# One projection slot fewer is shared: the left stage, the gates and the left rows move into other buffers

## The chip, the core and the metric

The kernel runs on one core of one Trainium2 chip. Its engines work side by side: PE (TensorE: matmuls, with PEld for its weight loads), DVE (VectorE), ACT (ScalarE), POOL (GpSimd) and SP (SyncE, which here only issues DMAs). SBUF is the large on-chip memory, PSUM the matmuls' own with 8 banks of 512 fp32 columns on 128 partitions. The metric is the device time of one execution in microseconds (us), the median of several runs; lower is better.

## The reference, cut to what matters

`x` has 2048 rows of 640, cut into 64 segments of 32 rows. A memory of 8 rows is handed from segment to segment:

```python
for s in range(64):
    h = concatenate([mem, x[32 * s:32 * s + 32]])      # 40 rows
    q, k, v = h @ Wq, h @ Wk, h @ Wv                   # 32 heads of 192
    p = softmax(where(mask, q @ k.T * 192 ** -0.5, -1e9))
    o = (p @ v) @ Wo
    mem, out_s = o[:8], o[8:]
a = concatenate(out)                                   # 2048 x 640
b = (gelu(x @ w_gate) * (x @ w_up)) @ w_down           # a feed-forward of its own
g = sigmoid((x * gate_w).sum(-1))
result = g * a + (1 - g) * b
```

Segment s + 1 can't begin its projections before segment s has produced `mem`. Wq, Wk, Wv are 640 x 6144, Wo is 6144 x 640, all in bf16.

## The kernel before, in words

**Stages.** The first 177 us compute the feed-forward `b` (kept in a scratch tensor in DRAM), the gates `g`, and load the attention's weights. Then come the 64 segments, one after the other, some 25 us each.

**Weights.** The weights are cut into pieces: Wq, Wk and Wv into 5 row blocks (k0 to k4) times 4 octets of heads, 384 KB each; Wo into 16 of 480 KB. Not all fit into SBUF. So 14 projection slots (`NSQ = 14`: Q's k1 to k4, K's and V's k0 to k4) and 3 Wo slots are shared by two pieces: that of octet 0 and that of octet 3. A segment with even s takes the octets in the order 0, 1, 2, 3, one with odd s in the order 3, 2, 1, 0. So what a segment uses last, the next one uses first; in between the first octet's pieces are replaced by the last octet's (`swap_loads`, L597 issues them on SP as soon as PE has read the old piece). "Octet i" below means the i-th that a segment takes. 17 such swaps run per segment, all on SP's queue in the order of the program.

**Left rows.** A segment's input on PE has 32 columns, but mem and rows are 40. The first 24 rows and the 8 memory rows are projected in the segment. The last 8 rows ("left" rows) of four segments, a group, are projected together as 32 rows, one group ahead: in segments with s % 4 = 0, 1, 2 stand "left units", each the Q and K projection of one octet (`lf`: matmuls, L882 for Q and L226 for K; `le`: evacuation, `left_rows`: ACT L887 copies the rows from PSUM to a buffer, DVE L889 transposes them, once for Q and once for K; `left_store`, L893, stores them to a DRAM scratch). Types 0 and 2 have one unit, type 1 has two. The segment of s % 4 = 3 projects left rows of V for the next group (`vb`). I call s % 4 the **type** of a segment. Groups run out at the end: segments 60 to 63 have no left units.

**One segment.** The order is written out by hand in a list, `PROG`: projections `g` (Q, K, V of octet i; L1039, and L226 where the weights already in PE serve again), row evacuations on ACT (L1059) and transposes on DVE (`tq`, `tk`, L1073), scores (`sc`: mask L1080, L1088, L1093), softmax (DVE L1107, L1109, ACT L1119, DVE L1121 to L1126), the transposes of p (`pt`, L1139 and L1144), P times V (`pv`, L1172 and L1174; evacuated by ACT L1183 into one of two head-output buffers `uT`), and the output projection `wo` (L1201; for the last octet L1224). ACT L1207 and DVE L1210 sum the halves of the first three octets' output. DVE L1340 adds the last octet's, and L1344 transposes the new memory rows into the next segment's input; PE's first L1039 of the next segment waits for it. POOL copies left rows of Q and K into the score operands before each octet (`left_fill`, L936 and L938) from the stage `stg`, which one DMA per segment fills (`stg_load`, L932, 192 KB, issued after the scores of octet 3). `mix` (POOL L963, L968, DVE L970) blends with `b` by the gates, held in SBUF (`gall`, `gallL`); `mix_left` (POOL L963, L976, DVE L978) does so for left rows, once per group, in the next type 0 segment.

**What orders the work.** Each operation declares the regions it reads and writes; a recording layer (`_Sched`) turns overlaps into semaphore waits. Every engine's stream, SP's too, runs in program order. For a region in PSUM (a whole bank) a read also waits for earlier reads by other engines.

## Time and profile before

| | |
|---|---|
| runs | 1800.49 us median of 3 (1795.53 to 1804.5) |
| profiled execution: span, first to last instruction | 1783.4 us |
| granted TensorE clock | 0.998 |
| segment 0 starts | 176.9 us |
| mean length of a segment of type 0, 1, 2, 3 (segments 4 to 62) | 25.07, 25.56, 23.90, 25.35 us |
| DMA bytes moved | 524.33 MB, 294 GB/s |

The page tells no other time of the profiled execution than its span. Lengths of segments are read off the timeline, from the first projection matmul (L1039) of one segment to that of the next. In the views of waits each line names the engine and line that stood idle, what ended the wait, the us in total, how often, and the longest. A line of the timeline gives start and duration in us, engine, line, what is written and read, how many instructions are merged, and in brackets the idle time before and what ended it.

### The profile page before, as it was taken

What the parts mean: (1) busy time and instruction counts of PE and PEld (TensorE: products, weight loads), DVE (VectorE), ACT (ScalarE), POOL (GpSimd) and SP (SyncE); (2) the same over time, 40 slices, a digit from 0 to 9 for tenths busy, and PEclk for the clock granted to TensorE, in tenths of its full rate; (3) what the DMA queues carried; (4) which work ended last, traced back from release to release, by engine and by line L of the source; (5) the groups of instructions that cost most, each with busy time, mean ns of one, the idle gap of its engine ahead of it and who ended that gap; (6) DMA issues with size and microseconds to landing.
All of it is one profiled execution on the core that took longest, in us unless ns stands there. A gap on an engine that the chain in (4) does not pass through costs nothing.

```text
span 1783.4 us, 80070 instructions
## 1 busy us (share of the span) xinstructions
PE 1629.5 (91%) x39162; PEld 817.9 (46%) x31501; DVE 957.7 (54%) x2932; ACT 793.8 (45%) x1835; POOL 319.8 (18%) x1099
## 2 busy tenths in 40 slices
PE   9999989899998999899899999899999989899987
PEld 4554444454444444454444444454444444454443
DVE  2223555555555655555565655555555655555554
ACT  3222444444444444444444444444444544444443
POOL 1100111111211111111111111111211111111211
PEclk9999999999999999999999999999999999999999
DMA  9815887888788887888788887888888887888786
GB/s 332 297 45 177 329 318 266 324 322 316 289 295 298 318 311 261 318 318 315 287 299 299 311 319 263 322 310 319 298 299 300 317 290 269 321 313 321 289 303 260
DMA packets 263390, 524.33 MB, mean 294 GB/s; under 512 B 97384, under 2 KB 116224, under 8 KB 263040
## 3 DMA queue, kind: packets, MB, share of 16 engines
q1 hardware_dynamic: 259912, 516.11, 79.5%
q8 instruction: 276, 4.52, 1.0%
q10 hardware_dynamic: 3128, 3.09, 0.5%
q14 instruction: 74, 0.61, 0.1%
HBM read 498.00 MB, written 21.11 MB: 291 GB/s over the span
## 4 chain that ended last, share of the span: by engine, by line
PE 69%; DMA 13%; DVE 8%; ACT 6%; issue 4%; SPq 0%; DVEq 0%; ACTq 0%
PE ps L1039 20%; PE ps L226 15%; PE ps L1201 8%; DMA arena<-in_A_Wv_dram 7%; PE ps L1172 3%; DMA left_qk_scratch<-arena 3%; PE ps L802 3%; PE ps L799 3%; PE ps L882 3%; DVE arena L889 3%; PE ps L1093 2%; PE ps L817 2%; ACT arena L887 2%; PE ps L1080 2%; PE ps L1088 2%
## 5 line engine op out<-in xcount | busy, mean ns | idle before, releaser
L1039 PE MATMUL ps<-arena 128*32 128x384 bf16 x9940 | 734.8, 328 | 58.5 <-DVE arena L1344 40.4
L226 PE MATMUL ps<-arena 128*32 128x384 bf16 x7680 | 584.4, 326 | 10.8 <-ACT arena L887 6.1
L1039 PEld LDWEIGHTS ps<-arena 128*32 128x32 bf16 x9940 | 254.0, 96 | 420.1 <-issue 244.4
L1073 DVE STREAM_TRANSPOSE arena<-arena 128x384 bf16<-128x384 bf16 x512 | 279.0, 564 | 227.0 <-ACT arena L1059 226.6
L1059 ACT ACTIVATE arena<-ps 128x384 bf16<-128x384 f32 x512 | 236.2, 489 | 176.3 <-PE ps L1039 164.4
L1201 PE MATMUL ps<-arena 128*32 128x320 bf16 x6144 | 297.0, 300 | 16.1 <-issue 15.5
L1201 PEld LDWEIGHTS ps<-arena 128*32 128x32 bf16 x6144 | 163.6, 97 | 75.7 <-issue 26.5
L1119 ACT ACTIVATE ps<-ps 104x160 f32<-104x160 f32 x256 | 74.3, 290 | 236.4 <-DVE ps L1109 236.4
L1107 DVE TENSOR_REDUCE arena<-ps 104x4 f32<-104x160 f32 x256 | 83.1, 325 | 176.0 <-PE ps L1093 175.7
L1157 ACT ACTIVATE arena<-ps 128x448 bf16<-128x448 f32 x192 | 104.8, 546 | 143.3 <-PE ps L1144 143.3
L1191 POOL COPY arena<-arena 128x96 bf16<-128x96 bf16 x256 | 68.4, 267 | 522.6 <-ACT arena L1183 419.3
L936 POOL COPY arena<-arena 128x96 bf16<-128x96 bf16 x256 | 70.0, 274 | 498.7 <-PE ps L1093 436.3
L1183 ACT ACTIVATE arena<-ps 128x480 bf16<-128x480 f32 (+1 forms) x256 | 138.1, 540 | 34.0 <-PE ps L1174 29.0
L1062 ACT ACTIVATE arena<-ps 128x384 bf16<-128x384 f32 x256 | 124.8, 488 | 52.7 <-PE ps L1039 52.4
L1172 PE MATMUL ps<-arena 128*64 128x160 bf16 x1536 | 122.1, 243 | 10.4 <-issue 3.4
L1172 PEld LDWEIGHTS ps<-arena 128*64 128x64 bf16 x1536 | 80.6, 109 | 97.9 <-ACT arena L1157 46.6
L882 PE MATMUL ps<-arena 128*32 128x384 bf16 x1280 | 111.1, 330 | 1.2 <-issue 1.2
L1174 PE MATMUL ps<-arena 128*64 128x64 bf16 x1536 | 105.1, 194 | 5.8 <-issue 5.8
L1121 DVE TENSOR_REDUCE arena<-ps 104x4 f32<-104x160 f32 x256 | 81.8, 320 | 51.6 <-ACT ps L1119 43.9
L889 DVE STREAM_TRANSPOSE arena<-arena 128x384 bf16<-128x384 bf16 x128 | 73.8, 577 | 57.4 <-ACT arena L887 52.6
L1224 PE MATMUL ps<-arena 128*32 128x160 bf16 x3072 | 77.1, 234 | 22.2 <-DMA arena<-in_A_Wo_dram 12.6
L887 ACT ACTIVATE arena<-ps 128x384 bf16<-128x384 f32 x128 | 62.4, 490 | 67.6 <-DVE arena L889 38.5
(84 smaller groups left out, 1816.7 us busy)
## 6 DMA issues: line engine op xcount, KB each, us to landing
arena<-in_A_Wk_dram SPq DMA_DIRECT2D x335, 384.0 KB, 7.7
arena<-in_A_Wv_dram SPq DMA_DIRECT2D x335, 384.0 KB, 9.4
arena<-in_A_Wq_dram SPq DMA_DIRECT2D x272, 384.0 KB, 5.6
arena<-in_A_Wo_dram SPq DMA_DIRECT2D x205, 480.0 KB, 7.4
left_qk_scratch<-arena SPq DMA_DIRECT2D x64, 192.0 KB, 2.6
arena<-left_qk_scratch SPq DMA_DIRECT2D x63, 192.0 KB, 7.8
ffn_b_scratch<-arena ACTq DMA_DIRECT2D x16, 160.0 KB, 3.7
arena<-ffn_b_scratch SPq DMA_DIRECT2D x64, 40.0 KB
```

The costliest lines, as they stand in the source:

```text
L226: return e.add_instruction(mybir.InstMatmult(name=nm, start_tensor_calc=like["start"], stop_tensor_calc=stop, tile_size=(128, 32), tile_po ...
L882: fns.append(lambda e, outp=outp, rhs=rhs, j=j: e.matmul(outp, lhs, rhs, start=(k == 0), stop=(k == KT - 1), tile_position=(0, 32 * j)))
L889: S_.add("dve", lambda e: e.transpose(out=dst[:, :, m].rearrange("p q c i -> p c q i"), in_=rowl.rearrange("p (c r) -> p c r", r=L)), read ...
L1039: fns.append(lambda e, outp=outp, rhs=rhs, j=j: e.matmul(outp, lhs, rhs, start=(k == 0), stop=(k == KT - 1), tile_position=(0, 32 * j)))
L1059: S_.add("act", lambda e, m=m, bk=bk: e.activation(out=rows_sb[m], in_=ps[:, bk, 0:384], func=ACTF.Copy), reads=[r_ps[bk]], writes=[r_rows ...
L1062: S_.add("act", lambda e, i=i, bk=bk: e.activation(out=v_sb[i % NVB].rearrange("p (c n) -> p c n", c=3), in_=ps[:, bk, 0:384].rearrange("p ...
L1073: S_.add("dve", lambda e: e.transpose(out=dst[:, :, 0:L], in_=rows_sb[m].rearrange("p (c r) -> p c r", r=L)), reads=[r_rows[m]], writes=[r ...
L1157: S_.add("act", lambda e: e.activation(out=PT, in_=ps[:, bank, 0:PTW + 128], func=ACTF.Copy), reads=[r_ps[bank]], writes=[r_PT], name="pT ...
L1172: return [lambda e: e.matmul(full, v[:, e0:e0 + 64], PTm[:, i], start=True, stop=False, tile_position=(0, 64 * i), skip_group_check=True), ...
L1174: lambda e: e.matmul(part, vl[:, e0:e0 + 64], PTl[:, i], start=False, stop=True, tile_position=(0, 64 * i), skip_group_check=True)]
L1183: S_.add("act", lambda e: e.activation(out=apx(u[:, 0, 0, :], [[R, na], [3 * R, 4], [1, R]]), in_=ps[:, A, 0:na * W].rearrange("p (c t r) ...
L1201: fns.append(lambda e, i=i, t=t, j=j, gv=gv: e.matmul(ps[32 * j:32 * j + 32, bank, 0:2 * DJ].rearrange("p (h n) -> p h n", h=2), lhs2[i], ...
```

## The change

- `NSQ` goes from 14 to 13: both pieces of Q's k1 are resident, and 13 projection pieces instead of 14 are swapped per segment. The room comes from the buffers below.
- The stage `stg` is gone. Its 192 KB are loaded in two halves of 96 KB into the two `uT` buffers: half 0 after the Wo matmuls of octet 2 (`("wo", 2, 1)`), half 1 at the very end of the segment, after the left store of type 0. The fills of octets 0 and 1 read half 0, those of 2 and 3 half 1.
- The gates `gall`, `gallL` lie in columns 384 to 479 of PSUM bank 7 instead of SBUF. `gate_cols` writes them with 3 transposes and 12 copies on DVE (before: 2 and 6). A new ACT copy per segment, `gate_now`, fetches the segment's column (in type 2 also the left group's) into SBUF; it stands after the evacuation of `pv` 3.
- The left rows' buffer `rowl` is gone. The rows pass through buffers that are idle just then (`spare_buf`); with the orders used, the second V buffer, and K's buffer for the K rows of type 0.
- The left inputs: one buffer `XL` for the Q and K units instead of two, and one, `XLx`, for V's left rows inside the last left-V buffer, so that each group's left x is loaded twice.
- `mix_left` is cut in two: POOL's part (`scale_left`) runs late in type 3, DVE's stays.
- `PROG` becomes four lists, one per type, which hold what the one list gave each type, in the same order.

The core of the diff:

```diff
-    NSQ = 14
+    NSQ = 13
...
+    def half_at(s_, h):
+        return wsB_off["uT"] + h * UB
+
+    def stage(s_, i):
+        o_ = i if s_ % 2 == 0 else NOCT - 1 - i
+        at = half_at(s_, i // 2) + 4 * LW * (o_ % 2)
+        return bview(at, 4 * LW).rearrange("p (m c i) -> p m c i", m=2, i=M), r_uT[i // 2]
...
-        for ga, ra, gi, ri in ((gall, r_gall, gin, r_gin), (gallL, r_gallL, ginL, r_ginL)):
-            S_.add("dve", lambda e, ga=ga, gi=gi: e.transpose(out=ga[0:32], in_=gi[0:32]), reads=[ri[0]], writes=[ra], name="gate T")
-            for j in range(1, 4):
-                S_.add("dve", lambda e, ga=ga, j=j: e.tensor_copy(out=ga[32 * j:32 * j + 32], in_=ga[0:32]), reads=[ra], writes=[ra],
+        for n, (gi, ri) in enumerate(((gin[:, 0:32], r_gin), (gin[:, 32:64], r_gin), (ginL, r_ginL))):
+            S_.add("dve", lambda e, gi=gi: e.transpose(out=gtmp[0:32], in_=gi[0:32]), reads=[ri[0]], writes=[r_gtmp], name="gate T")
+            for j in range(4):
+                S_.add("dve", lambda e, n=n, j=j: e.tensor_copy(out=ps[32 * j:32 * j + 32, GB, GC + 32 * n:GC + 32 * n + 32], in_=gtmp[0:32]),
+                       reads=[r_gtmp], writes=[r_ps[GB]], name="gate copy")
...
-    def stg_load(s):
-        S_.add(AUXQ, lambda e: e.dma_start(stg_flat, qkl[s]), reads=[Rg("qk", NSEG * i + s, NSEG * i + s + 1) for i in range(NOCT)],
-               writes=r_stg, dma_sem="stg", name="stg s%d" % s)
+    def stg_load(s, h):
+        o0 = 2 * ((h + s) % 2)
+        at = half_at(s, h)
+        S_.add(AUXQ, lambda e: e.dma_start(bview(at, 8 * LW), qkl[s][:, 2 * LW * o0:2 * LW * (o0 + 2)]),
+               reads=[Rg("qk", NSEG * i + s, NSEG * i + s + 1) for i in (o0, o0 + 1)],
+               writes=[r_uT[h]], dma_sem="stg%d" % h, name="stg s%d" % s)
...
+    def gate_now(s):
+        two = s % 4 == 2
+        col = ps[:, GB, GC + s:GC + s + 1]
+        at = bass.AP(col.tensor, col.offset, [list(col.ap[0]), [NSEG + s // 4 - s, 2]]) if two else col
+        S_.add("act", lambda e: e.activation(out=gcur[:, 0:1 + two], in_=at, func=ACTF.Copy), reads=[r_ps[GB]],
+               writes=r_gcur[0:1 + two], name="gate s%d" % s)
...
+    gate_at = [max(("pv", NOCT - 1), ("wo", 2, 1), key=prog.index) for prog in PROGS]
...
+    def spare_buf(x):
+        at = (wsB_off["uT"] + UB, wsB_off["v"] + 768, wsB_off["K"], wsB_off["uT"])[x]
+        return bview(at, 768), sreg(at, 768)
...
-        elif s + 1 < NSEG:
-            stg_load(s + 1)
...
+            if item == gate_at[q]:
+                gate_now(s)
             swap_loads(s, item)
+            if item == ("wo", 2, 1) and s + 1 < NSEG:
+                stg_load(s + 1, 0)
...
+            if n == nqkv and q == 3:
+                scale_left(g)
...
             wo_left(s, held)
             if s + 1 == NSEG:
                 left_sums(g)
+        if s + 1 < NSEG:
+            stg_load(s + 1, 1)
```

## The prediction, on record before the changed kernel ran

> **What bounds the kernel now.** I read the page first (which engine is full), then TensorE's own waits, then the timeline around one segment's end, then the SP queue with its landings.

> ```profile
> PE 1629.5 (91%) x39162; PEld 817.9 (46%) x31501; DVE 957.7 (54%) x2932; ACT 793.8 (45%) x1835; POOL 319.8 (18%) x1099
> ...
> arena<-in_A_Wq_dram SPq DMA_DIRECT2D x272, 384.0 KB, 5.6
> ...
> arena<-left_qk_scratch SPq DMA_DIRECT2D x63, 192.0 KB, 7.8
> ```

> TensorE (PE) is busy 91% of 1783.4 us, so about 150 us of idle time is all that edits off PE can win. Its waits say where:

> ```profile
> PE ps L1039 <- DVE arena L1344: 40.4, 48, 1.8
> ...
> PE ps L1224 <- DMA arena<-in_A_Wo_dram: 12.6, 22, 0.9
> PE ps L1039 <- DMA arena<-in_A_Wv_dram: 9.3, 19, 1.6
> ...
> PE ps L1039 <- DMA arena<-in_A_Wk_dram: 3.5, 11, 0.6
> ```

> Columns: us in total, times, longest. 40.4 us are the hand-over between segments (L1344 transposes the new memory into the next input). Swapped weights cost 12.6 + 9.3 + 3.5 = 25.4 us: all that a lighter swap stream can give back directly. By the landings they fall in types 1 and 2 (s % 4), hardly in 3, never in 0, where weights land 0.7 us early or more.

> Not all of the 25.4 is on the path. Here is the end of segment 29 (type 1), ACT's rows and DVE's:

> ```profile
> 925.81 0.44 ACT L1183 ACTIVATE arena<-ps 128x320 bf16<-128x320 f32 x1 [0.19 <-PE ps L1174]
> 926.36 0.49 ACT L887 ACTIVATE arena<-ps 128x384 bf16<-128x384 f32 x1
> 927.57 0.49 ACT L887 ACTIVATE arena<-ps 128x384 bf16<-128x384 f32 x1 [0.71 <-DVE arena L889]
> ```

> ```profile
> 925.72 0.67 DVE L1210 TENSOR_TENSOR arena<-ps,arena 64x160 f32<-64x160 f32 x2 [0.97 <-PE ps L1174]
> 926.32 0.31 DVE L1188 CAST arena<-ps 128x160 bf16<-128x160 f32 x1
> 926.96 0.58 DVE L889 STREAM_TRANSPOSE arena<-arena 128x384 bf16<-128x384 bf16 x1 [0.33 <-ACT arena L887]
> 928.16 0.58 DVE L889 STREAM_TRANSPOSE arena<-arena 128x384 bf16<-128x384 bf16 x1 [0.63 <-ACT arena L887]
> 928.66 0.21 DVE L1340 TENSOR_TENSOR arena<-ps,arena 128x64 bf16<-128x64 f32 x1
> 928.91 0.25 DVE L1344 STREAM_TRANSPOSE arena<-arena 128x64 bf16<-128x64 bf16 x1
> ```

> The left rows go ACT L887, DVE L889, again L887, again L889, each waiting for the one before; only then can DVE take L1340, and L1344 lets PE start at 929.21. Where segments have left units (0 to 59), types 1 and 2 end by this chain, not by the last Wo matmul: the second L889 ends 0.1 to 1.3 us after it in all 28 looked at (segments 4 to 59).

> **The change, part by part.**

> *One swap fewer, 63 times.* V pieces k0 to k4 of type 2 land 14.45, 15.45, 16.47, 17.53 and 18.66 us after the segment's start: 1.05 us apiece. So K, V and Wo land up to 1.05 us earlier, less 0.26 (a quarter of it) for the 96 KB stage half now issued just ahead, and in type 1 less 0.4 more: there SP is still held by the left store of type 0, the first swap goes out 1.57 us into the segment, and the half's issue (0.4, as L932's now) comes before it. That leaves 0.8 in types 2 and 3, 0.4 in type 1. What it is worth, gap by gap:
> - Wk 3.5: 0.5 of it stands in type 2 ahead of the pT matmul of octet 2 (L1139), where PE waits for the softmax anyway. 3.0 counts.
> - Wv 9.3: the gaps before piece k3 are followed by pT of octet 3. Taken away, PE comes to it earlier and waits for DVE L1125. Each gap counts only as far as pT now starts late against its operand; summed, 5.3.
> - Wo 12.6: the piece is late for the last Wo matmuls, which end ahead of the chain above. 0 counts; the wait becomes a longer one for L1344.

> Gain 8.3, bounds 0 and 25.4. 8.3 is nearest to what the rows show to be uncovered.

> *The gate on ACT, 64 times.* It stands right behind the uT evacuation of octet 3 (L1183) and reads bank 7, so it waits for the second L1210; behind it are queued the L887 of the chain, and for that waits everything up to PE. L1210 ends at 926.39; DVE to ACT takes 0.03 (L889 ends 927.54, L887 starts 927.57). The nearest row for its length is L747 (128x40, 0.20). ACT instructions that wait for nothing start 0.11 before the end of the one ahead (rows evacuations L1059: two in 0.87, each 0.49). So L887 starts at 926.51 instead of 926.36, or at 926.64 without the overlap: 0.15 to 0.28. In type 2 L887 stands later against L1210, and it is 0.10 to 0.23. In type 0 L887 waits for PE longer than the gate lasts, in type 3 there is none: 0. Over 15 segments each: 15 x 0.25 = 3.8, without the overlap 15 x 0.51 = 7.7. I take 3.8, since such neighbours overlap. [...]

> *Gate columns into PSUM, once.* Eight DVE instructions become 15 (three transposes, twelve copies into bank 7).

> ```profile
> 178.25 0.74 DVE L739 COPY arena<-arena 32x64 f32<-32x64 f32 x3
> 179.03 0.20 DVE L737 STREAM_TRANSPOSE arena<-arena 32x32 f32<-32x32 f32 x1
> 179.26 0.59 DVE L739 COPY arena<-arena 32x32 f32<-32x32 f32 x3
> ```

> At 0.20 each, 15 from 178.03 end at 181.05. In the changed order the first K matmul of octet 1 in segment 0 waits for the last copy, since it writes bank 7; now it runs at 178.94 (L226). PE loses 2.1; scores come 2.1 later too, so the transposes queued on DVE behind the copies are ready for them. Bounds 1.7 (0.173 us each, a copy's own mean) and 3.6 (0.325, the nearest row that writes PSUM, L924). [...]

> *At nothing, with their cover.* The first stage half waits for the Wo matmuls of octet 2, which end 21.5, 21.3, 19.7 and 21.1 us into types 0 to 3, of 25.1, 25.6, 23.9 and 25.4. Its copies must be over when scores start at 3.20 of the next segment and take 0.6: 6 us from issue to landing are free. It is no longer queued behind the swaps (Wo lands by 22, in type 1 by 24); the left store, 192 KB in a quiet queue, takes 2.6. The second half is issued at the segment's end, in type 0 1.5 later, and is needed at 7.5. The uT evacuation of octet 1 now waits for the last left fill, which ends 0.35 or more before it. Left rows pass through V's second buffer (PV 3 has left it 0.65 before) and K (the next Kl copy waits 0.35 longer, scores 1.7 later still). The Pool half of the left mix moves off the start of type 0, where L978 waits 8.3 us for it, but PE doesn't wait there: 0. The second x load adds 40 KB every fourth segment behind V.

> **Sum:** -8.3 + 3.8 + 2.1 = -2.4 us, span 1783.4 to 1781.0. The timed runs (median 1800.49, 1795.53 to 1804.5) lie 12 to 21 us above that span; the page gives no other time of the profiled execution, so I take the difference off the median: **1798.1 us**.

> **Rivals.**
> - *The lighter stream gives all.* The chain before L1344 moves up with Wo, because rows that I count as fixed only follow PE. For it: PE feeds this chain. Against: the chain's own four steps take 2.4 us. -25.4 + 3.8 + 2.1 = -19.5: 1781.
> - *Slower: the gate serialises ACT in the chain*, and the stage half takes the swap's place. It decides from 0.25 us per segment. 7.7 + 3.6 for the start and no gain: +11.3, 1812. For it: the chain ends types 1 and 2 without slack. Against: neighbours on ACT overlap.
> - *Slower: the stage comes late.* Before, it took 7.8 us to land, against 6 free: at 7.8 scores wait 1.8 us in 63 segments, +113, 1911. Against: the 7.8 is its place behind the swaps.
> - *It doesn't do what it says*: the changed order has 63 swap issues fewer, so this is out.

> **How the numbers follow.** Forecast with small errors on either side 0.56; all given back 0.23; gate serial 0.16; stage late 0.05. A measurement of this kernel can tell about 0.5% (9 us) from no change. So: faster 0.23, within 0.56, slower 0.21. The range takes most of the way to the first two rivals and leaves out the stage: 1783 to 1811.

> **What would show it.** Wq issues 272 to 209. Wk and Wv waits of PE nearly gone, Wo's too, while L1039 <- L1344 grows by about Wo's share; L1139 <- DVE grows by some 4 us. A new ACT group 128x1 x64 near 0.19 us, L887 behind it 0.1 to 0.3 later against L1210. One PE gap near 179 us of about 2 us, ended by DVE. Type 2 shorter by 0.1 to 0.3, type 1 within 0.2, types 0 and 3 unchanged. I am wrong if types 0 or 3 change by more than 0.2, if L936 waits for a DMA, or if L1344's wait falls.

## The result, and the profile after

The changed kernel takes 1787.63 us (median of 20 runs, 1778.59 to 1796.88); the kernel before, on the same chip, 1796.91 us (20 runs, 1790.02 to 1804.5). Ratio 0.9946, interval 0.9929 to 0.9964: 9.7 us faster (6.5 to 12.8). On another chip the ratio was 0.9917, interval 0.9888 to 0.9946 (below). The forecast was 2.4 us faster, 1798.1. The time lies in the range; the sign is right, the size is short by 7 us.

The two profiled executions alone would have told another story: spans 1783.4 and 1782.5. Each of these 20 runs of the changed kernel comes with its span, and the span is 1.8 to 2.0 us below its time. So nothing like 12 to 21 us lies around the span: the first profile was one of the shortest among executions that scatter by some 15 us. A second profile of the same kernel before has a span of 1795.2.

The page of the changed kernel (busy time of each engine; DMA issues with KB each and us to landing):

```profile
PE 1626.4 (91%) x39181; PEld 820.6 (46%) x31501; DVE 959.1 (54%) x2939; ACT 800.6 (45%) x1899; POOL 321.0 (18%) x1099
...
arena<-in_A_Wq_dram SPq DMA_DIRECT2D x209, 384.0 KB, 5.3
...
arena<-left_qk_scratch SPq DMA_DIRECT2D x126, 96.0 KB, 2.3
```

63 Q loads fewer, and a stage half lands in 2.3 us instead of 7.8 for the whole: its slack of 6 us is never used up, and no wait of the fills (now L977) is put down to a DMA. TensorE's waits in the changed kernel (us in total, times, longest; L1433 is the former L1344, L1190 the former L1139, L1275 the former L1224):

```profile
PE ps L1092 <- DVE arena L1433: 50.4, 48, 1.8
...
PE ps L1190 <- DVE arena L1176: 11.6, 32, 0.9
PE ps L1275 <- DMA arena<-in_A_Wo_dram: 7.2, 14, 1.0
...
PE ps L1092 <- DMA arena<-in_A_Wv_dram: 2.8, 6, 0.9
...
PE ps L1092 <- DMA arena<-in_A_Wk_dram: 1.2, 2, 1.0
```

Late weights fell from 25.4 to 11.2 us, and 10.0 of that came back in the wait for the next input (40.4 before): the cover that the prediction described. Of what is left, 9.2 us stand in type 1 and 2.0 in type 2.

### The profile page after: what moved, and what is told of

Read it like the earlier page. It is cut to its first block, busy times and chain, and to the rows that moved or that the text cites. A ratio compares the mean times of both kernels' runs of the same rounds, so it can differ in the third digit from the quotient of the medians.

```text
span 1782.5 us, 80354 instructions
## 1 busy us (share of the span) xinstructions
PE 1626.4 (91%) x39181; PEld 820.6 (46%) x31501; DVE 959.1 (54%) x2939; ACT 800.6 (45%) x1899; POOL 321.0 (18%) x1099
## 5 line engine op out<-in xcount | busy, mean ns | idle before, releaser
L1092 PE MATMUL ps<-arena 128*32 128x384 bf16 x9940 | 734.4, 328 | 61.4 <-DVE arena L1433 50.4
L226 PE MATMUL ps<-arena 128*32 128x384 bf16 x7680 | 586.7, 326 | 13.3 <-ACT arena L920 6.6
L1112 ACT ACTIVATE arena<-ps 128x384 bf16<-128x384 f32 x512 | 236.2, 489 | 180.2 <-PE ps L1092 171.9
L977 POOL COPY arena<-arena 128x96 bf16<-128x96 bf16 x256 | 69.6, 272 | 535.2 <-PE ps L1146 427.2
L1115 ACT ACTIVATE arena<-ps 128x384 bf16<-128x384 f32 x256 | 124.9, 488 | 63.2 <-PE ps L1092 63.1
L922 DVE STREAM_TRANSPOSE arena<-arena 128x384 bf16<-128x384 bf16 x128 | 73.8, 577 | 58.8 <-ACT arena L920 55.5
L1160 DVE TENSOR_TENSOR ps<-ps,arena 104x160 f32<-104x160 f32 x256 | 85.1, 332 | 8.8
L1275 PE MATMUL ps<-arena 128*32 128x160 bf16 x3072 | 72.8, 234 | 13.1 <-DMA arena<-in_A_Wo_dram 7.2
## 6 DMA issues: line engine op xcount, KB each, us to landing
arena<-in_A_Wk_dram SPq DMA_DIRECT2D x335, 384.0 KB, 7.1
arena<-in_A_Wv_dram SPq DMA_DIRECT2D x335, 384.0 KB, 9.1
arena<-in_A_Wq_dram SPq DMA_DIRECT2D x209, 384.0 KB, 5.3
left_qk_scratch<-arena SPq DMA_DIRECT2D x64, 192.0 KB, 2.2
```

What stands on the lines that cost most here:

```text
L226: return e.add_instruction(mybir.InstMatmult(name=nm, start_tensor_calc=like["start"], stop_tensor_calc=stop, tile_size=(128, 32), tile_po ...
L1092: fns.append(lambda e, outp=outp, rhs=rhs, j=j: e.matmul(outp, lhs, rhs, start=(k == 0), stop=(k == KT - 1), tile_position=(0, 32 * j)))
L1112: S_.add("act", lambda e, m=m, bk=bk: e.activation(out=rows_sb[m], in_=ps[:, bk, 0:384], func=ACTF.Copy), reads=[r_ps[bk]], writes=[r_rows ...
L1115: S_.add("act", lambda e, i=i, bk=bk: e.activation(out=v_sb[i % NVB].rearrange("p (c n) -> p c n", c=3), in_=ps[:, bk, 0:384].rearrange("p ...
L1160: S_.add("dve", lambda e: e.tensor_tensor(out=S3, in0=S3, in1=mxb, op=ALU.subtract), reads=[rb, rst], writes=[rb], name="smax sub")
```

## The experiments

All ratios are to the kernel before on the same chip, with their intervals. The changed kernel's own two ratios, from two chips, differ by 0.003 (5 us), and the four runs from the late store to the first try at the start have no changed kernel timed beside them, so a difference of that size to it shows nothing there. Theory A: the lighter stream gives the gain, and the relocations take part of it back. Theory B: a relocation gives the gain.

**The kernel before, once more.**

> The kernel before, unchanged, as one more measurement with a second profile. If the first profiled execution (span 1783.4) was only a fast one among executions that scatter, the runs here list spans about 1.9 us below their times, scattered over some 14 us, and the second profile has another span, by up to 10 us, with the difference in the same lines as between fast and slow executions (stalls that no wait explains, DMA landings). If instead some 12 to 21 us lie outside the span in a timed run, spans stand near 1783 while times stand near 1797. Ratio 1.000 within 0.0015.

1795.60 us (12 runs), ratio 1.0011 (0.9992 to 1.0029), spans 1.7 to 1.9 below the times. The second profile differs from the first in places that no edit touched: type 2 is 0.43 us longer per segment, type 3 0.25, Wk waits 8.1 instead of 3.5. Differences of a few tenths per segment between two single profiles prove nothing by themselves.

**One slot fewer in the kernel before.** The 63 loads of Q's k1 are left out, so of octets 0 and 3 one multiplies by the other's piece (one octet of four, not two as the expectation has it); nothing is relocated.

```diff
         for key in done_keys:
             other = swap_in.get(key)
...
+            if other[0] == 0 and other[2] == 1:
+                loaded[slot_id[other]] = other
+                continue
             load_piece(other, "swap s%d" % seg)
```

> The kernel before with the 63 swap loads of Q's piece k1 left out and nothing else changed, so two of the four octets' Q products use the wrong piece k1 (that part of the computation is wrong). Theory A: faster than before by 8.3 (the sum on record) to 16 us (the timed gain plus what the relocations cost), ratio 0.991 to 0.9955, segments of type 1 and 2 shorter by 0.2 to 0.5 us each. Theory B: within 3 us of before, ratio 0.998 to 1.002.

1772.79 us, ratio 0.9884 (0.9857 to 0.9912): 21 us faster, more than A expected (8.3 to 16) and far from B. Its waits:

```profile
PE ps L1042 <- DVE arena L1347: 54.2, 48, 1.8
...
PE ps L1142 <- DVE arena L1128: 12.5, 38, 0.8
...
PE ps L1227 <- DMA arena<-in_A_Wo_dram: 1.5, 4, 0.8
```

The same two kinds of wait in the second profile of before:

```profile
PE ps L1039 <- DVE arena L1344: 43.2, 48, 1.8
...
PE ps L1224 <- DMA arena<-in_A_Wo_dram: 12.1, 19, 1.1
```

Against that profile (span 1795.2 to 1770.5, so 24.7 us less) TensorE waits 24.5 us less for swapped weights (26.7 to 2.1) and 18.9 more for other engines (hand-over, p, left rows): a net of 5.6, where the prediction has 8.3. TensorE's busy time falls by 12.2, of which some 7 are half clock (last section: four windows of 3.4 us fewer). The stalls that end with no releaser ("issue") fall by 6.2, but these scatter from 27 to 39 us among the traces with swaps, whatever the number of slots, so no part of them can be put down to one slot.

**The slot taken back in the changed kernel.**

```diff
-    NSQ = 13
+    NSQ = 14
```

> The changed kernel with 14 shared projection slots again instead of 13: all relocations stay (stage in the head-output buffers, gates in bank 7, left rows through the V and K buffers), only the swap of Q's piece k1 comes back. Theory A (the gain of about 10 us is the lighter swap stream, less what the gate on ScalarE and the start cost): slower than the kernel before by 3 to 8 us (3.8 + 2.1 forecast), so ratio 1.002 to 1.004, and the waits on Wk, Wv and Wo are back at about 25 us. Theory B (the gain comes from a relocation, such as the stage half that no longer queues behind the swaps, and the one swap is worth little): still faster than before by 5 to 10 us, ratio 0.994 to 0.997.

1809.16 us, ratio 1.0075 (1.0045 to 1.0105): the relocations alone cost 13.5 us, twice the 5.9 of the prediction; B falls. The waits for weights are 48 us, where A expected 25, and 25 of them stand in type 1. The two places that grew: type 1 segments (26.12 us against 25.59 in the second profile of before, 8.5 us over 16), and the start (segment 1 begins at 210.0 instead of 204.7). The longest wait for Wv, 5.1 us, is the start, in segment 0:

```profile
PE ps L1275 <- DMA arena<-in_A_Wo_dram: 19.9, 28, 1.4
PE ps L1092 <- DMA arena<-in_A_Wv_dram: 17.8, 31, 5.1
```

The trace shows this only in part: its execution was the fastest of the eight (1798.72). Over all eight, TensorE lost 11.1 us to half clock on average (one minus the granted clock, times the span), against 7.4 in the 19 runs of before, so 3.7 of the 13.5 us lie there.

**No swaps at all.** As the diff of the run with one slot fewer, with `if True`: every shared slot keeps its first piece, so half of the shared products use another octet's weights.

> The kernel before with all swap loads left out (every shared slot keeps its first piece, so half of the shared products use wrong weights): the most that any lightening of the stream can give. If the waits on weights all lie on the path: faster by 25 to 35 us, ratio 0.981 to 0.986. If, as the prediction has it, the Wo waits lie beside the chain of left rows and most of the Wv waits ahead of the pT wait: faster by 8 to 14 us, ratio 0.992 to 0.9955, with the hand-over wait of L1344 and the pT wait grown by the rest.

1724.95 us, ratio 0.9619 (0.9593 to 0.9646): 70 us, twice the larger expectation, although late weights were 25 to 27 us of waits. First a part of the page and two rows of its waits, then the same of the second profile of before:

```profile
PE 1602.4 (93%) x39162; PEld 812.7 (47%) x31501; DVE 956.0 (55%) x2932; ACT 792.4 (46%) x1835; POOL 319.2 (19%) x1099
...
q8 instruction: 276, 4.52, 1.1%
```

```profile
PE ps L1042 <- DVE arena L1347: 56.9, 48, 1.6
PE ps L1142 <- DVE arena L1128: 16.0, 49, 0.8
```

```profile
PE 1633.8 (91%) x39162; PEld 817.3 (46%) x31501; DVE 957.1 (53%) x2932; ACT 793.6 (44%) x1835; POOL 319.5 (18%) x1099
...
q8 instruction: 276, 4.52, 1.0%
```

```profile
PE ps L1201 <- issue: 16.5, 20, 1.4
PE ps L1174 <- issue: 6.7, 9, 1.4
```

The rows of TensorE's waits put down to "issue" sum to 39.1 us in the second profile of before (36.4 in the first), and there is none without swaps, with the same 276 instruction packets on q8. So they are a price of the swap stream as a whole. Whether these packets queue behind the weights was not tried. Busy time falls by 31 us. Half clock, below, counts as busy, and five windows of it fewer make some 8.5 us; where the other 23 come from no run shows.

**The left store moved behind three swaps.** In type 0 the store of left rows is the last thing that SP is given; in the next segment it holds all swaps until its rows are ready.

```diff
         if m:
-            left_store(*unit(s, u), 3)
+            if n > n_wos[s % 4]:
+                held_store.append(unit(s, u))
+            else:
+                left_store(*unit(s, u), 3)
...
             swap_loads(s, item)
+            if item == ("g", 0, 3) and held_store:
+                left_store(*held_store.pop(), 3)
```

> The changed kernel with the left store that type 0 leaves to SP at its end issued in the next segment behind the swap of Q's piece k3 instead of ahead of all swaps. Theory A: in type 1 the first swap goes out about 1 us into the segment instead of 2.27, all later pieces land 1.0 to 1.3 earlier, type 1's waits on weights (some 10 of the 12.2 us that the changed kernel still has) go, and type 1 gets 0.2 to 0.5 us shorter: 3 to 8 us faster than the changed kernel, ratio to the kernel before 0.990 to 0.993. Rival (type 1 ends by the chain of left rows, so that the Wo waits only turn into the hand-over wait): only the K and V waits count, 0 to 3 us, ratio 0.993 to 0.9946.

1774.95 us, ratio 0.9917 (0.9899 to 0.9935): 5 us under the changed kernel's first ratio, as A expected, but level with its second (below), so the times alone don't decide. The trace does. SP's queue at the start of segment 29 in the changed kernel (begins at 904.11), then in this one (902.10):

```profile
905.31 0.37 SPq L926 DMA_DIRECT2D left_qk_scratch<-arena  x1
905.72 0.51 SPq L971 DMA_DIRECT2D arena<-left_qk_scratch  x1
906.27 0.44 SPq L630 DMA_DIRECT2D arena<-in_A_Wk_dram  x1
```

```profile
901.51 0.33 SPq L971 DMA_DIRECT2D arena<-left_qk_scratch  x1
902.65 0.38 SPq L630 DMA_DIRECT2D arena<-in_A_Wk_dram  x1
...
904.02 0.43 SPq L926 DMA_DIRECT2D left_qk_scratch<-arena  x1
```

The first swap goes out 0.55 us into the segment instead of 2.16, and waits for weights in all fall from 11.2 to 5.6 us, those in type 1 (9.2) go altogether, and the hand-over wait grows from 50.4 to 55.0. Type 1 is 0.36 us shorter than in the changed kernel (0.24 against its second profile). The store, with the same bytes, costs by its place in the queue.

**Four gates instead of one, and the gate elsewhere.**

```diff
             if item == gate_at[q]:
-                gate_now(s)
+                for _ in range(4):
+                    gate_now(s)
```

> The changed kernel with the gate copy on ScalarE issued four times in a row instead of once. By the prediction's rule every one adds 0.10 us (overlapped) to 0.19 us (not) to the chain that ends types 1 and 2, in 30 segments: three more cost 9 to 17 us, ratio to the kernel before 0.9995 to 1.004, and the hand-over wait grows in types 1 and 2 alone. If ScalarE has slack there, under 3 us, ratio 0.994 to 0.996; then the gate was not worth 3.8 us either.

1807.55 us, ratio 1.0104 (1.0082 to 1.0126): 28 us over the changed kernel, above the 9 to 17 expected. The second L922 ends 0.51 us later against L1261 in type 1 and 0.63 in type 2 (14 segments each), 0.17 to 0.21 per extra gate, which is no overlap: some 17 us over 30 segments. Most of the rest is half clock (last section), in eleven places against one. It took 21.7 us of the six timed runs on average, and 7.2 of the changed kernel's twenty.

```diff
-    gate_at = [max(("pv", NOCT - 1), ("wo", 2, 1), key=prog.index) for prog in PROGS]
+    gate_at = [("ex", 1) for prog in PROGS]
```

> The changed kernel with the gate copy taken out of the chain at the end of the segment: it stands behind the exponentials of octet 1, when bank 7 is not in use and ScalarE waits for the next projection. By the prediction's 3.8 us: ratio to the kernel before 0.992 to 0.993, L920 behind it 0.15 us earlier against L1261 in types 1 and 2. If the gate is hidden: within 1 us of the changed kernel, ratio 0.994 to 0.995; if it delays the rows of the next projection instead: slower by 1 to 4 us.

1776.27 us, ratio 0.9932 (0.9911 to 0.9953): no measurable difference to the changed kernel. Segment 29 of the changed kernel, ACT:

```profile
926.41 0.44 ACT L1234 ACTIVATE arena<-ps 128x320 bf16<-128x320 f32 x1
927.02 0.17 ACT L1010 ACTIVATE arena<-ps 128x1 f32<-128x1 f32 x1 [0.17 <-DVE arena L1261]
927.09 0.48 ACT L920 ACTIVATE arena<-ps 128x384 bf16<-128x384 f32 x1
928.27 0.49 ACT L920 ACTIVATE arena<-ps 128x384 bf16<-128x384 f32 x1 [0.69 <-DVE arena L922]
```

The gate lasts 0.17 and the next row overlaps it by 0.10, as forecast. Against the second profile of before the first L920 starts 0.12 later after L1261 in type 1, but the second L922 only ends 0.03 later (2.56 against 2.53), in type 2 0.02. But more than the gate differs from that kernel. Against the run with the early gate, where only the gate moved, the second L922 of the changed kernel's two profiles ends 0.11 and 0.10 later in type 1 (2.56 and 2.54 against 2.45), 0.02 and 0.09 in type 2: 1.8 to 2.6 us over these 28 segments. So the first gate does reach the chain. The comparison with before hides it, because there the stretch from the first left copy to the end of the second transpose is some 0.1 longer in type 1 (2.55 against 2.44); why is open.

**The start, twice.** The stall that both tries are to remove, in the changed kernel:

```profile
182.93 0.33 PE L226 MATMUL ps<-arena 128*32 128x384 bf16 x4 [2.19 <-DVE ps L772]
```

Gate columns are written while the last feed-forward block runs, and the x load of left group 1 is to be issued later: behind the Wo pieces in the first try, behind the first five Wv pieces in the second. The diff is of the second.

```diff
-    gate_cols()
-    if NG > 1:
-        xl_load(1, XL, r_XL, "xl0")
...
+            if blk + 1 == NFB and a == 2:
+                gate_cols()
...
     load_residents(3, lambda key: key[0] < 3 and not on_tmp(key))
+    if NG > 1:
+        xl_load(1, XL, r_XL, "xl0")
```

> The changed kernel with two things of its start put elsewhere: the gate columns are written into bank 7 while the last feed-forward block still runs (VectorE is idle there), and the x load of left group 1 is issued behind the resident weights of segment 0 instead of ahead of them. Theory A (the relocations' cost is in places that can be named; at the start it is the 2.2 us stall on the last gate copy, 1.7 us of half clock that follows it near 184 us, and Wv pieces issued 3.4 us later): 3 to 5 us faster than the changed kernel, ratio to the kernel before 0.992 to 0.993, no gap over 1 us near 181 us and no clock below 0.99 in segment 0. If another wait takes its place (the Wv pieces of segment 0, as in the run with 14 slots): within 1 us of the changed kernel, ratio 0.994 to 0.995.

1784.40 us, ratio 0.9975 (0.9956 to 0.9994), slower than the changed kernel's 0.9946 if anything. A miss of my own making: left products of segment 0 need this load, and TensorE stood 6.5 us for it.

```profile
PE ps L1252 <- DMA arena<-left_x_scratch: 6.5, 1, 6.5
```

> As the first start experiment, but with the x load of left group 1 issued behind the first five Wv pieces instead of behind the Wo pieces, so that it lands before its left products (they waited 6.5 us for it there). Theory A: the 2.2 us stall on the gate copies and the half clock behind it (1.7 us) go: 3 to 4 us faster than the changed kernel, ratio 0.9920 to 0.9935 if the changed kernel stands at 0.9946. Rival (the resident weights of segment 0, which land one after the other until 202 us, bound the start anyway): within 1 us of the changed kernel.

1787.11 us, ratio 0.9945 (0.9924 to 0.9966): no measurable gain, as the rival has it. But this try moved the gate columns only. The `load_residents` call that the x load was put behind issues nothing with 13 slots, so the load still goes out ahead of every Wv piece, as in the changed kernel (180.07, the first Wv at 181.91):

```profile
179.49 2.00 SPq L741 DMA_DIRECT2D arena<-left_x_scratch  x1
181.52 0.91 SPq L630 DMA_DIRECT2D arena<-in_A_Wv_dram  x2
```

What it shows: the 2.2 us stall is gone, 1.4 us of Wo waits follow at 203 to 205, and segment 1 begins at 206.2 instead of 207.8 and 206.8 in the changed kernel's two profiles (204.1 and 204.7 before). With both pieces of Q's k1 resident, five Wo pieces stand ahead of Wv at the start instead of four; the changed kernel's last resident Wo piece lands at 201.95 instead of 198.93. In the first try, where the x load did move, the first Wv was issued at 179.06 and that piece landed at 200.60. So the x load explains some of the delay at most, and no run shows what a start without it and without the 6.5 us stall would give.

**The changed kernel once more, all three edits together (of the start's, with 13 slots only the gate columns take effect), and these without the slot.**

> The changed kernel, unchanged, as one more measurement on the chip of the next three, with a second profile. Ratio 0.993 to 0.9965 (0.9946 so far). If the scatter from run to run is the half-clock episodes (TensorE at half clock for 3.4 us where about 1.7 us of idle time falls into one window of a fixed 3.41 us grid), the profile shows another number of them than the one at 184 us, and the runs' times follow their mean clocks at about 1.8 us per 0.001.

> The changed kernel with the late left store, the early gate and the mended start together. If the three prices add (5 + 2 + 3.5 us): 9 to 12 us faster than the changed kernel, ratio to the kernel before 0.988 to 0.990. If two of them shorten the same waits: ratio 0.990 to 0.992, about that of the late store alone (0.9917).

> As the last, but with 14 shared slots: the relocations without their three known costs and without the lighter stream. If these three (the store ahead of the swaps of type 1, the start, the gate) are what the relocations cost (1.0075 with them): ratio to the kernel before 0.998 to 1.002. If their cost lies elsewhere (a busier DMA queue by the two stage halves, the left rows through V and K): ratio 1.004 to 1.008.

The changed kernel: 1781.51 us, ratio 0.9917 (0.9888 to 0.9946). All three edits: 1775.96 us, ratio 0.9872 (0.9837 to 0.9907), by the ratios 8 us under the changed kernel on the same chip (the intervals just overlap) and the lowest of the versions that leave nothing out. Its waits for weights are 3.0 us. The same with 14 slots: 1792.34 us, ratio 0.9965 (0.9946 to 0.9983), faster than before, and by the ratios 19.8 us below the relocations as they were made (some 5 of it half clock: 5.7 us of these runs on average against 11.1). So their 13.5 us do lie in these places, and by the traces in the store's above all: in type 1 the waits for weights fall from 24.9 to 2.4 us and the segment from 26.12 to 25.39, 11.7 us over 16, while the start still waits 4.3 us for Wv (5.1) and segment 1 begins at 208.8 (210.0). The kernel before has the store ahead of its swaps too (12 us of waits for weights in type 1), which would be why the mended one beats it; before with the late store alone was not run. The slot by itself, 0.9872 against 0.9965, is again worth some 17 us.

That the times follow the mean clock at 1.8 us per 0.001 holds in part: over 169 runs, each against its kernel's mean, the slope is 1.4 us and the correlation -0.57.

## Why the prediction was right in kind and short in size

- *What bounds the kernel*: TensorE and the hand-over chain. Right: late weights fell by 14 us, the wait for the next input grew by 10. The Wo waits did not nearly go, though: 7.2 us are left, for the reason under *Type 1*.
- *One swap fewer, 8.3 us*: the mis-sized term. Measured alone it is 21 us, or 17 with the mended relocations. The cover was there and even a little larger (net of waits 5.6 in that profile), but only rows of waits for weights were counted. More than half of the 21 us carry no weight's name: 4.1 are half clock by the timed runs (3.3 us lost on average against 7.4), and for the rest the cause stays open (less busy time, and perhaps fewer issue stalls). The bound of 25.4 for what a lighter stream can give back directly was no bound for the time: the whole stream is worth 70.
- *Type 1, 0.4 us less*: mis-sized. The stage half's issue takes 0.71 there on average (0.32 in type 0's segments), so the first swap goes out at 2.40 instead of 1.62 into the segment, 0.78 later. That eats the 0.8 that type 1 should have kept.
- *Gate, 3.8 us*: somewhat too dear; 1.8 to 2.6 us by the chain's end against the early gate (0.10 to 0.11 per segment in type 1 for the 0.15 forecast, 0.02 to 0.09 in type 2 for 0.10), the duration and overlap as forecast. The timed runs can't tell so little.
- *Gate columns, 2.1 us*: the stall came as forecast, 2.19, but taking it away gained nothing that the times show: then Wo is waited for. What was overlooked is SP: behind a fifth Wo piece and the x load, Wv's issue starts at 181.9 instead of 178.5. And the stall had a sequel, last section.
- *At nothing, with their cover*: right. The first stage half lands 2.5 us or more (4.1 in the median) before its scores need its copies, and no fill waits for it. The issue of the second one is not free (see *Type 1*).
- *From span to median*: wrong. A span lies 1.7 to 2.1 us below its own run's time in all timed runs that list both; the rest was scatter.
- *The sum*: -21 (slot) and +13.5 (relocations) against -8.3 and +5.9. Both terms were short by a factor above two and in opposite directions, so their sum missed by 7 us only. That it came so near is luck.
- *Signs to look for*: Wq x209, L1190 +4, the gap near 179 and the ACT group came true. Type 1 stayed within 0.2 as forecast (0.19 longer); type 2 did not get shorter by 0.1 to 0.3 (0.02 longer, or 0.41 shorter against the second profile of before). One sign of being wrong did come up: types 0 and 3 were to change by no more than 0.2, and type 0 fell by 0.23 and type 3 by 0.26. For type 3 two profiles of the kernel before differ by as much (0.25), for type 0 only by 0.08. Type 0 is as short with the slot taken back (24.83), so it does not need the lighter stream; the cause is open.

## What to carry to other kernels

Price a transfer stream by leaving it out, whole or in part, before summing waits: here the whole stream was worth 70 us and its rows of waits 25. When DMA issues change, read each queue in order at the place where it is held by a wait, because what is queued behind it pays, not the transfer itself (here the first swap of segment 29 went out 2.16 us into it with the left store ahead, 0.55 us without); and read it again after an edit that is to move one, for the edit may move nothing. And take two profiles of the unchanged kernel before reading tenths of a microsecond per segment.

## What the runs showed of the hardware

```profile
180.60:184.00 3.40, 1.21 (x32) 1.00 1.12 304
184.00:187.40 3.40, 3.40 (x58) 0.50 1.00 351
```

```profile
574.80:578.20 3.40, 1.73 (x50) 1.00 1.03 391
578.20:581.60 3.40, 3.40 (x64) 0.52 0.73 276
```

The page's row of tenths hides this (every slice reads 9). Each window of 3.4 us costs about 1.7 us (half of it, an estimate), and it counts as busy. The thirteen traces with swaps hold 38 episodes, one to eleven in each, besides the end of the program (its last 25 us); the kernel without swaps has none. They begin on a fixed grid of windows that are as long as a single episode, 3.413 us: in the second profile of before the later three start 17.0, 47.0 and 339.0 windows after the first. The window of the grid ahead of each held 1.56 us or more of idle TensorE. Of the 6465 other windows on the grid at full clock (from 160 us on, all traces), 105 held as much, and none more than 2.03. Windows that lie across the grid held up to 2.36 without one, so whether a stall trips it depends on where it falls, and that differs from run to run: part of the scatter. In a window of the grid, 1.56 to 2.03 us of idle TensorE, in one stall or in several, had half clock after it in some cases, more than 2.03 us in every case.
